# Batch 0's copies, batch 1's scalings and accumulators, and one more filler product in a fused retention and swish kernel

## The chip, the cores and the metric

The kernel runs on one core of a Trainium2 chip. The metric is the device time of one execution in microseconds (us), the median of several runs. Before the change it is 296.62 us over 3 runs (296.17 to 297.3).

Engine names: PE is the matrix engine (PEld its weight loads), DVE, ACT and POOL the vector, scalar and GpSimd engines, SP the engine that issues most DMA. PE writes to PSUM, which has eight banks here divided by tag: three `mm`, two `O`, two `sc`, one `st`.

## The reference

Retention over 8 batches, 8 heads, 576 positions and head size 64, and then a feed-forward with a swish of learned slope:

```
scores = (q @ k^T) / sqrt(64)
gamma[h] = 1 - 2**(-5 - h)
D[h, i, j] = gamma[h]**(i - j) if i >= j else 0
attn = (scores * D) @ v                    # [8, 8, 576, 64]
x = attn.transpose(0, 2, 1, 3).reshape(4608, 512)
h = x @ w_in                               # [4608, 2048]
g = h / (1 + exp(-beta * h))               # beta: one value for each of 2048 columns
out = g @ w_out                            # [4608, 512], float32
```

## The kernel before

**What is computed how.** The decay is split: q is multiplied by gamma**i / 8 (`gq`), v by gamma**-j (`gv`, `gvh`). Positions are taken in chunks of 64. Within a pair of chunks the scores are products of q and k, masked to the causal triangle on DVE (the tiles `R`), then multiplied with v. What lies before a chunk comes in through a state, the running sum of products of k and v (`st` in PSUM, `sbd`, `sbq` and `end` in SBUF). Products of the state with q ("cross" products) are added in the same PSUM tile `O`. The copy of `O` into `xT` is the input of the feed-forward, transposed as PE wants it.

**Blocks.** Each batch gives a block of 512 rows; the last 64 positions of all batches make a ninth block. For each block come `up` (16 groups `fo` of 4 products, then a Silu with slope beta on ACT into `gT`) and `down` (4 row groups `ms` of 16 products, then a copy to `ot` and a store). The Silu of beta * h is beta times too large, so `w_out` is multiplied by 1 / beta (`rbeta_sb`) when it is cast to bfloat16. Before that `betas_safe` (L251) adds 1e-12 to each beta whose square is under 1e-24, in three tiny operations; `tiny` shares its tile with `rbeta_sb`.

**Batch 0** has functions of its own (`pre_q`, `t_q`, `pre_s`, `s_T`, `s_sc`, `s_st`, `s_keep`, `s_O`, `s_cross`, `s_x`), called in the order written out near the end. DVE scales q; PE transposes it; POOL copies or scales k and v, four loads of each; PE transposes k and makes the scores; DVE masks them (L402, eight in all). `s_keep(a, n, ...)` copies a state from PSUM into `sbds[n]` for the head half a, two casts a call, and `s_x(a, hh, e)` copies `O` to `xT` on engine e. Products of the identity with itself (`keep_warm`, L241) and of zeros (`warm_up`) are fillers whose results nobody reads.

**Batch 1** has functions that begin with `o_` and works in two spans of 256 positions, each with heads in two halves a = 0, 1. `o_pre(s, j, a)` makes kn (j = 0) or vn (j = 1), `o_T` transposes kn in PSUM and copies it to kT, `o_sc` makes scores and masks, `o_st(c)` a state's products, `o_keep(c, st)` adds it to the sum before it (L624) and casts that for PE (L629), `o_out` makes the outputs and copies them to xT. Later batches use functions that begin with `d_`, and POOL scales their q.

**Order.** Each engine takes its instructions strictly in the order in which the program emits them. From block 0's feed-forward on, that order is made by `merged`: `fill` is the list of feed-forward steps, and each stream holds (place in `fill`, step) pairs that are put in between. `d0` is the place of block 0's first `down`, `u1` that of block 1's first `up`. There `first_ups` makes two groups with two accumulators in `mm`, and `up(1, 2, ...)` follows with a third. The streams place `pre_q(1, n)`, `t_q(1, u)` and `o_pre` at d0 + 7 to d0 + 12.8, `first_span` at d0 + 14 and `first_out` at d0 + 15.9. `cast_w_in` and `cast_w_out` cast the weights as they land; `rest` holds batch 0's last cross products and copies.

The functions that the change touches, with the line numbers of the profile:

Of the kernel before, what the change touches and what calls it, by code (L numbers as in the profile page):

```python
# [11 lines left out]
F32 = mybir.dt.float32  # L12
BF16 = mybir.dt.bfloat16
ACT = mybir.ActivationFunctionType
ALU = mybir.AluOpType
# [4 lines left out]
def kernel(  # L20
# [10 lines left out]
    nc = tc.nc  # L31
# [4 lines left out]
    P = 128  # L36
# [92 lines left out]

    warm = consts.tile([P, 256], F32, name="warm")  # L130
    first = consts.tile([P, 256], F32, name="first")
    nc.vector.memset(warm[:], 0.0)

    pos = consts.tile([P, 3, CB + 1], F32, name="pos")
    for j, (step, mul) in enumerate(((1, CB), (P, 1))):
# [96 lines left out]
    for g in range(2, NP):  # L232
        load_w_in(g)

    def warm_up(n, cols=256, tag="mm"):
        ph = psum.tile([P, MB], F32, name="ph", tag=tag, bufs=3 if tag == "mm" else 1)
        for _ in range(n):
            src = warm[:].unsqueeze(1).to_broadcast([P, 2, 256]) if cols > 256 else warm[:, :cols]
            nc.tensor.matmul(ph[:, :cols], warm[:, :P], src, start=True, stop=True,
                             skip_group_check=True)  # L240

    def keep_warm(tag="mm"):
# [8 lines left out]

    def betas_safe():

        nc.gpsimd.tensor_tensor(tiny[:], beta_sb[:], beta_sb[:], ALU.mult)
        nc.gpsimd.tensor_scalar(tiny[:], tiny[:], 1e-24, 1e-12, ALU.is_lt, ALU.mult)
        nc.gpsimd.tensor_tensor(beta_sb[:], beta_sb[:], tiny[:], ALU.add)

# [18 lines left out]
    def pre_q(b, n):  # L278

        if n == 0:  # L280
            batch[b] = dict(qs=sb.tile([P, CB, H, D], BF16, name="qs", tag="qs", bufs=2),
                            qT=sb.tile([P, CB, HP, P], BF16, name="qT", tag="qT", bufs=2))
        if b < 2:
            hs, cs = slice(n // 2 * HP, (n // 2 + 1) * HP), slice(n % 2 * 2, n % 2 * 2 + 2)
            for to, hs in [(hs, hs)] if n < 2 or b < QB else turned[1:]:
                nc.vector.tensor_tensor(batch[b]["qs"][:, cs, to], q_tiles[b][:, hs, cs].rearrange("p h i d -> p i h d"),
                                        gq[:, cs, hs].unsqueeze(3).to_broadcast([P, 2, len(range(H)[hs]), D]), ALU.mult)
        else:
            if n % 2:
                return  # L290
            cs = slice(n, n + 2)
            for to, hs in turned:
                nc.gpsimd.tensor_tensor(batch[b]["qs"][:, cs, to], q_tiles[b][:, hs, cs].rearrange("p h i d -> p i h d"),  # L293
                                        gq[:, cs, hs].unsqueeze(3).to_broadcast([P, 2, len(range(H)[hs]), D]), ALU.mult)
# [265 lines left out]
        return lambda: cross(1), evict  # L560


    def o_pre(s, j, a, e=None):

        w, S, e = slice(a * HP, (a + 1) * HP), span_of(1, s), e or nc.gpsimd
        src = span_tiles[1, s, j].rearrange("p h i d -> p i h d")
        if j:
            e.tensor_tensor(S["vn"][:, :, w], src[:, :, w],
                            gvh[:, 2 * s:2 * s + 2, w].unsqueeze(3).to_broadcast([P, 2, HP, D]), ALU.mult)
            return  # L570
        for to, hs in turned[1:] if a else turned[:1]:
            e.tensor_copy(S["kn"][:, :, to], src[:, :, hs])  # L572

    def o_T(s, tags, es):

        S, ts = spans[1, s], []
        for a in range(2):
            if a < len(tags):
                T = psum.tile([P, 2 // len(tags), 2, 2, P], BF16, name="T", tag=tags[a], bufs=3 if tags[a] == "mm" else 2)
            t = T[:, a if len(tags) == 1 else 0]  # L580
            for i in range(2):
                for pl in range(2):
                    nc.tensor.transpose(t[:, i, pl, :], heads(S["kn"][:, i], 2 * a + pl), ident[:])
            ts.append(t)
        for a in range(2):
            es[a](S["kT"][:, :, 2 * a:2 * a + 2], ts[a])
# [19 lines left out]
                    nc.vector.tensor_tensor(S["R"][a][:, j], sc[a][j][:], causal_span[:].unsqueeze(2).to_broadcast([P, 2, 2, P]), ALU.mult)  # L606
        return masks

    def o_st(c):

        S, hh = spans[1, c // 2], c % 2
        st = psum.tile([P, HP, D], F32, name="st", tag="st", bufs=1)
        for i in range(2):
            for p in range(HP):
                for j in range(2):
                    nc.tensor.matmul(st[half(j), p, :], S["kn"][half(hh), i, 2 * p + j, :], S["vn"][half(hh), i, head_of(1, p, j), :],
                                     start=i == 0 and p == 0, stop=True, skip_group_check=True)
        return st
# [12 lines left out]
    def o_out(s):  # L631

        S, seen = spans[1, s], set()
        O = {(hh, y): psum.tile([P, 2, P], F32, name="O", tag="sc" if y else "O", bufs=2) for y in range(2) for hh in range(2)}

        def to(hh, p, x):
            first, o = (hh, p // 2, x) not in seen, O[hh, p // 2][half(x), p % 2, :]
            seen.add((hh, p // 2, x))
            return o, first

        def own(hj):
            for i in range(2):
                for pp in range(2):
                    for y in range(2):
                        for hh, j in hj:
                            p = pp + 2 * y
                            h = head_of(1, p, j)
                            o, first = to(hh, p, h % 2)
                            m = nc.tensor.matmul(o, S["vn"][half(hh), i, h, :], S["R"][y][half(hh), j, i, pp, :],  # L649
                                                 start=first, stop=True, skip_group_check=True)  # L650
                            held_back.append(m)
            return m

        def cross(cj):
            for pp in range(2):
                for y in range(2):
                    for hh, j in cj:
                        c, p = 2 * s + hh, pp + 2 * y
                        o, first = to(hh, p, j ^ y)
                        m = nc.tensor.matmul(s_view(o), sbq[2 * c - 1][half(j), p, :], o_q(c, half(j), p),  # L660
                                             start=first, stop=True, skip_group_check=True)
                        held_back.append(m)
            return m

        def fence(last):
            f = nc.vector.memset(fenced[:], 0.0)
            after(f, last)
            held_back.clear()
            return f

        held_back = []
        if s == 0:
            f = fence(cross([(1, 0), (1, 1)]))
            st = o_st(1)
            own([(0, 0), (0, 1), (1, 1)])
            held_back.clear()
            own([(1, 0)])
        else:
            f = fence(own([(0, 1), (1, 0)]))
            own([(0, 0), (1, 1)])  # L680
            st = o_st(3)
            cross([(0, 0), (1, 1)])
            held_back.clear()
            cross([(0, 1), (1, 0)])
        for m in held_back[:2 + 2 * s]:
            after(m, f)

        def evict():
            for n, ((hh, y), o) in enumerate(O.items()):
                c = 2 * s + hh  # L690
                (dve, act)[n % 2](xt(1)[:, 2 * y:2 * y + 2, :, c * PC:(c + 1) * PC], o.rearrange("k p (i w) -> k p i w", i=CB))
        return evict, st
# [36 lines left out]
    def down(m, ms, f0, fn=4, n0=0, nn=d_model):  # L729
# [3 lines left out]
            pos_[ms] = psum.tile([P, d_model], F32, name="po", tag="mm" if m or ms < 3 else "st", bufs=3 if m or ms < 3 else 1)  # L733
        po = pos_[ms]
        for fo in range(f0, f0 + fn):
            parts = ((0, nn),) if m > 1 or CB * fo + ms < (56 if m else 50) else ((0, nn // 2), (nn // 2, nn))
            for x, y in parts:
                nc.tensor.matmul(po[:, x:y], gT[:, fo, ms, :], w_out_sb[:, fo, n0 + x:n0 + y],  # L738
                                 start=(fo == 0), stop=(fo == FO - 1), skip_group_check=m < 2)
# [28 lines left out]
    def F(f, *a):  # L768
        return lambda: f(*a)
# [1 line left out]

    whole_span, low, high = slice(0, P), half(0), half(1)

    warm_up(2, MB)
    betas()
    betas_safe()
    pre_q(0, 0)
    pre_q(0, 1)
    t_q(0, 0)
# [36 lines left out]
    s_x(0, 0, act)  # L816
    s_cross(3, 0)
    s_st(1, 1, 0, low)
    s_x(0, 1, act)
    s_keep(1, 0, (dve, dve), 1)  # L820
    s_st(1, 0, 1, low)
    s_keep(1, 2, (dve, dve), 0)
    s_O(0, 1, "sc")
    s_O(1, 1, "sc")
    cast_w_in(0, (0, 1), (1,))
    cast_w_in(1, (0, 1), (1,))
    cast_w_in(0, (2, 3), (3,))
# [63 lines left out]
    def first_out():  # L891
        evict, st = o_out(0)
        evict()
        o_T(1, ("mm",), (act, dve))
        o_keep(1, st)

    def second_span():
        masks = o_sc(1)
# [9 lines left out]
    def triangles():  # L908
        for t, pattern in zip(tri, ([[1, CB], [CB, TL // CB]], [[1, TL]])):
            nc.gpsimd.memset(t[:], 1.0)  # L910
            for x in range(2):
# [11 lines left out]
                (d0 + 13.6, F(x_k, XB, 0)),  # L923
                (base[2] - 4.5, F(release, 4)), (base[2] + 10, F(release, 4))],
               [(d0 + 7, F(pre_q, 1, n)) for n in range(4)] + [(d0 + 12.5, F(pre_q, XB, n)) for n in range(4)] + [(d0 + 11.6, F(t_q, 1, 0)), (d0 + 11.6, F(t_q, 1, 1))],
               [(d0 + 8, F(o_pre, 0, 0, 0)), (d0 + 8, F(o_pre, 0, 0, 1)), (d0 + 9, F(o_pre, 0, 1, 0)),
                (d0 + 12.7, F(o_T, 0, ("O", "sc"), (dve, act))), (d0 + 12.8, F(o_pre, 0, 1, 1, nc.vector)),
                (d0 + 14, first_span), (d0 + 15.9, first_out)],
               [(d0 + 10, F(o_pre, 1, 0, 0)), (d0 + 10, F(o_pre, 1, 0, 1)), (d0 + 12, F(o_pre, 1, 1, 0)), (d0 + 12, F(o_pre, 1, 1, 1)),
# [89 lines left out]
```

## Time and profile before

| | |
|---|---|
| median of 3 runs | 296.62 us (296.17 to 297.3) |
| the profiled execution | 296.88 us |
| its span, first to last instruction | 295.1 us |
| PE busy in it | 289.5 us, 3404 products |
| DVE, ACT, POOL busy | 103.1, 145.7, 110.0 us |
| DMA | 53.99 MB, 183 GB/s in the mean |

How to read what follows. The profile is a page of one execution, with views that can be asked for. A line of a timeline is: start and length in us, engine, line of the kernel, operation, tile written<-tiles read, shapes, how many were merged (x8), and in brackets the idle time of the engine before it and what ended that. In the chain of waits, followed back from the last instruction, a line is start, length, and what the time went to. In the list of waits: who waited, for whom, us in total, times, longest. Ends of PE's instructions are modelled, so lines of one engine can overlap by some tenths.

### The profile page before, as it was taken

Reading aid. Unit: us, or ns where it says so; the run is one execution under the profiler, and the core shown is the slowest. Engines: PE = TensorE matmul, PEld = TensorE weight load, DVE = VectorE, ACT = ScalarE, POOL = GpSimd, SP = SyncE. Lnnn points to the kernel's source line nnn. Section 1 sums busy time; section 2 is a strip of 40 time slices with the busy share of each in tenths; the row PEclk is TensorE's granted clock in tenths of the full one; section 3 lists DMA queues with packets and bytes.
Section 4 is the critical chain, followed back from the end, with each engine's and each line's share of the span. In section 5 each row is a group of like instructions: output and inputs, shape, how many; then the busy total and the mean of one; then the engine's idle time right before and its main releaser. Section 6 shows DMA issues by size and latency. Waiting matters only on the chain.

```text
span 295.1 us, 7955 instructions
## 1 busy us (share of the span) xinstructions
PE 289.5 (98%) x3404; PEld 150.0 (51%) x3404; DVE 103.1 (35%) x219; ACT 145.7 (49%) x260; POOL 110.0 (37%) x218
## 2 busy tenths in 40 slices
PE   7999999999999999999999999999999999999995
PEld 3654467875544454455445544554554544444443
DVE  5765566505630651055204520354053500110012
ACT  5566537892377334743473348434770167007600
POOL 5956037945904614271229405764323000000000
PEclk9999999999999999999999999999999999999999
DMA  7999999999999799939999939999997110131011
GB/s 224 305 368 384 378 301 276 213 180 235 198 216 259 188 162 244 252 59 160 211 252 215 187 105 266 183 183 199 210 165 143 73 38 0 36 71 38 0 71 71
DMA packets 119938, 53.99 MB, mean 183 GB/s; under 512 B 93648, under 2 KB 112352, under 8 KB 119904
## 3 DMA queue, kind: packets, MB, share of 16 engines
q1 hardware_dynamic: 119872, 53.49, 81.0%
q8 instruction: 26, 0.43, 0.6%
q14 instruction: 8, 0.07, 0.1%
q10 hardware_dynamic: 32, 0.01, 0.0%
HBM read 36.71 MB, written 9.44 MB: 156 GB/s over the span
## 4 chain that ended last, share of the span: by engine, by line
PE 95%; ACT 1%; DMA 1%; DVE 0%; issue 0%; DVEq 0%
PE po L738 43%; PE ph L703 38%; PE ph L718 4%; PE O L531 2%; PE sc L485 1%; PE O L544 1%; PE st L503 1%; DMA qn<-in_q_dram 1%; PE T L346 1%; ACT sbd L453 1%; PE ph L244 1%; PE sc L399 0%; PE sc L600 0%; PE T L379 0%; ACT xT L425 0%; PE O L649 0%
## 5 line engine op out<-in xcount | busy, mean ns | idle before, releaser
L738 PE MATMUL po<-w_out_sb,gT 128*128 128x512 bf16 (+3 forms) x614 | 128.7, 366 | 0.0
L705 ACT ACTIVATE gT<-ph,beta_sb 128x512 bf16<-128x512 f32 (+1 forms) x143 | 91.1, 645 | 49.2 <-PE ph L703 48.8
L703 PE MATMUL ph<-xT,w_in_sb 128*128 128x512 bf16 (+1 forms) x572 | 113.7, 359 | 0.5 <-ACT gT L872 0.5
L738 PEld LDWEIGHTS <-gT 128*128 128x128 bf16 x614 | 58.0, 98 | 62.8
L703 PEld LDWEIGHTS <-w_in_sb 128*128 128x128 bf16 x572 | 55.5, 98 | 56.1 <-issue 0.8
L745 DVE COPY ot<-po 128x512 f32<-128x512 f32 (+2 forms) x33 | 22.2, 672 | 72.8 <-PE po L738 72.8
L293 POOL TENSOR_TENSOR qs<-qn,gq 128x256 bf16<-128x256 f32 (+1 forms) x36 | 26.3, 757 | 34.2 <-DMA qn<-in_q_dram 33.8
L492 DVE TENSOR_TENSOR R<-sc,tri 128x512 bf16<-128x512 f32 x28 | 17.4, 683 | 60.0 <-PE sc L485 60.0
L322 POOL CAST kn<-kvn 128x128 bf16<-128x128 f32 (+1 forms) x72 | 20.9, 328 | 34.2 <-DMA kvn<-in_k_dram 34.1
L300 POOL TENSOR_TENSOR vn<-kvn,gv 128x512 bf16<-128x512 f32 x24 | 25.0, 1041 | 7.7 <-DMA kvn<-in_v_dram 7.5
L559 ACT CAST xT<-O 128x512 bf16<-128x512 f32 x14 | 7.5, 588 | 32.2 <-PE O L544 32.2
L514 ACT CAST sbd<-warm 128x256 bf16<-128x256 f32 x18 | 7.3, 405 | 25.5 <-DVE warm L511 20.7
L718 PE MATMUL ph<-xT,w_in_sb 128*128 128x512 bf16 x56 | 12.9, 379 | 0.1
L511 DVE TENSOR_TENSOR first<-st,warm 128x256 f32<-128x256 f32 x24 | 10.2, 425 | 2.5
L511 DVE TENSOR_TENSOR warm<-st,first 128x256 f32<-128x256 f32 x18 | 7.6, 422 | 9.6 <-PE st L503 8.4
L559 DVE CAST xT<-O 128x512 bf16<-128x512 f32 x14 | 9.0, 686 | 5.1 <-PE O L544 5.1
L721 ACT ACTIVATE gT<-ph,beta_sb 128x512 bf16<-128x512 f32 x14 | 8.6, 686 | 4.2 <-PE ph L718 4.2
L310 POOL TENSOR_TENSOR kn<-tln,gq 128x128 bf16<-128x128 f32 (+1 forms) x12 | 5.6, 470 | 11.8 <-DMA tln<-in_q_dram 7.0
L210 POOL CAST w_in_sb<-wt 128x256 bf16<-128x256 f32 (+1 forms) x15 | 7.9, 540 | 5.0 <-DMA wt<-in_moe_w_in_dram 4.9
L718 PEld LDWEIGHTS <-w_in_sb 128*128 128x128 bf16 x56 | 5.3, 97 | 6.4 <-issue 0.5
L514 ACT CAST sbd<-first 128x256 bf16<-128x256 f32 x18 | 7.3, 405 | 2.3 <-DVE first L511 0.3
L572 POOL CAST kn<-kvn 128x256 bf16<-128x256 f32 (+1 forms) x6 | 2.9, 516 | 13.3 <-DMA kvn<-in_k_dram 13.3
(117 smaller groups left out, 176.6 us busy)
## 6 DMA issues: line engine op xcount, KB each, us to landing
qn<-in_q_dram SPq DMA_DIRECT2D x16, 512.0 KB, 5.9
kvn<-in_k_dram SPq DMA_DIRECT2D x32, 256.0 KB, 5.9
kvn<-in_v_dram SPq DMA_DIRECT2D x32, 256.0 KB, 5.5
out_dram<-ot SPq DMA_DIRECT2D x31, 256.0 KB, 3.6
wt<-in_moe_w_out_dram SPq DMA_DIRECT2D x8, 512.0 KB, 8.8
wt<-in_moe_w_in_dram SPq DMA_DIRECT2D x5, 512.0 KB, 10.2
wt<-in_moe_w_in_dram SPq DMA_DIRECT2D x6, 256.0 KB, 5.7
tln<-in_q_dram SPq DMA_DIRECT2D x8, 128.0 KB, 3.6
```

The lines of the kernel that those rows point to most:

```text
L293: nc.gpsimd.tensor_tensor(batch[b]["qs"][:, cs, to], q_tiles[b][:, hs, cs].rearrange("p h i d -> p i h d"), gq[:, cs, hs].unsqueeze(3).to_ ...
L300: nc.gpsimd.tensor_tensor(live[i]["vn"], kv_tiles.pop(i)[:, 1], gains(gv, c), ALU.mult)
L322: nc.gpsimd.tensor_copy(kn[:, c % 2, to], t[:, 0, hs])
L492: nc.vector.tensor_tensor(R[x][:, j].rearrange("k c p q -> k (c p) q"), sc[x, j].rearrange("k c p q -> k (c p) q"), mask, ALU.mult)
L511: nc.vector.tensor_tensor(new[:], add, sums[(c - 1) % 2][:], ALU.add)
L514: nc.scalar.copy((sbq[c] if c < NC - 1 else ends[u])[:], new[:])
L559: (nc.scalar.copy if n % 2 else nc.vector.tensor_copy)(x, o)
L703: nc.tensor.matmul(ph, w_in_sb[:, ko, fo * P:(fo + 1) * P], xts[m][:, ko, :, w], start=(ko == 0), stop=(ko == KO - 1))
L705: nc.scalar.activation(gts[m][:, fo, :, w], ph, ACT.Silu, scale=beta_sb[:, fo:fo + 1])
L718: nc.tensor.matmul(phs[f][:], w_in_sb[:, ko, f * P:(f + 1) * P], xts[m][:, ko], start=(ko == 0), stop=(ko == KO - 1))
L738: nc.tensor.matmul(po[:, x:y], gT[:, fo, ms, :], w_out_sb[:, fo, n0 + x:n0 + y], start=(fo == 0), stop=(fo == FO - 1), skip_group_check=m < 2)
L745: (nc.scalar.copy if m == 0 else nc.vector.tensor_copy)(ot, po[:, :nn])
```

## The change

- The warm-up operand is cleared and read in its first 128 columns alone, repeated four times; the product has the same size.
- Behind the transpose of beta stands one more `keep_warm`, where `betas_safe` was called. `betas_safe` goes from POOL to DVE, and to a later place, behind batch 0's last `s_O`.
- In batch 0 `s_x(0, 1)` goes from ACT to DVE, and `s_keep(1, 2)` from DVE to ACT.
- In batch 1 the last quarter of q's scaling (`pre_q(1, 3)`, two operations) goes from DVE to POOL. Of `o_pre(0, 1, 1)`, which DVE did whole, POOL does two of the four heads and DVE the others.
- `o_T` of the second span writes to the bank `st` instead of an `mm` bank, and `o_st(1)` to an `mm` bank instead of `st`. In `first_out`, `o_keep(1, st)` now comes ahead of that `o_T`.
- In block 1's `down`, the products of group fo = 14 for ms = 0 and 1 are no longer split into two of 256 columns.

```diff
@@ -129 +129 @@
-    nc.vector.memset(warm[:], 0.0)
+    nc.vector.memset(warm[:, :P], 0.0)
@@ -232 +232 @@
-    def warm_up(n, cols=256, tag="mm"):
-        ph = psum.tile([P, MB], F32, name="ph", tag=tag, bufs=3 if tag == "mm" else 1)
+    def warm_up(n):
+        ph = psum.tile([P, CB, P], F32, name="ph", tag="mm", bufs=3)
         for _ in range(n):
-            src = warm[:].unsqueeze(1).to_broadcast([P, 2, 256]) if cols > 256 else warm[:, :cols]
-            nc.tensor.matmul(ph[:, :cols], warm[:, :P], src, start=True, stop=True,
+            nc.tensor.matmul(ph[:], warm[:, :P], warm[:, :P].unsqueeze(1).to_broadcast([P, CB, P]), start=True, stop=True,
                              skip_group_check=True)
@@ -251 +250 @@
     def betas_safe():
-        nc.gpsimd.tensor_tensor(tiny[:], beta_sb[:], beta_sb[:], ALU.mult)
-        nc.gpsimd.tensor_scalar(tiny[:], tiny[:], 1e-24, 1e-12, ALU.is_lt, ALU.mult)
-        nc.gpsimd.tensor_tensor(beta_sb[:], beta_sb[:], tiny[:], ALU.add)
+        nc.vector.tensor_tensor(tiny[:], beta_sb[:], beta_sb[:], ALU.mult)
+        nc.vector.tensor_scalar(tiny[:], tiny[:], 1e-24, 1e-12, ALU.is_lt, ALU.mult)
+        nc.vector.tensor_tensor(beta_sb[:], beta_sb[:], tiny[:], ALU.add)
@@ -283 +282 @@
-                nc.vector.tensor_tensor(batch[b]["qs"][:, cs, to], q_tiles[b][:, hs, cs].rearrange("p h i d -> p i h d"),
+                e = nc.gpsimd if b and n == 3 else nc.vector
+                e.tensor_tensor(batch[b]["qs"][:, cs, to], q_tiles[b][:, hs, cs].rearrange("p h i d -> p i h d"),
@@ -560 +560 @@
-    def o_pre(s, j, a, e=None):
-        w, S, e = slice(a * HP, (a + 1) * HP), span_of(1, s), e or nc.gpsimd
+    def o_pre(s, j, a, e=nc.gpsimd):
+        S, w = span_of(1, s), slice(a * HP + (2 if e is nc.vector else 0), (a + 1) * HP - (2 if e is not nc.vector and s == 0 and a else 0))
@@ -576 +576 @@
-                T = psum.tile([P, 2 // len(tags), 2, 2, P], BF16, name="T", tag=tags[a], bufs=3 if tags[a] == "mm" else 2)
+                T = psum.tile([P, 2 // len(tags), 2, 2, P], BF16, name="T", tag=tags[a], bufs=1 if tags[a] == "st" else 2)
@@ -606 +606 @@
-    def o_st(c):
+    def o_st(c, tag="st"):
-        st = psum.tile([P, HP, D], F32, name="st", tag="st", bufs=1)
+        st = psum.tile([P, HP, D], F32, name="st", tag=tag, bufs=3 if tag == "mm" else 1)
@@ -671 +671 @@
-            st = o_st(1)
+            st = o_st(1, "mm")
@@ -733 +733 @@
-            parts = ((0, nn),) if m > 1 or CB * fo + ms < (56 if m else 50) else ((0, nn // 2), (nn // 2, nn))
+            parts = ((0, nn),) if m > 1 or CB * fo + ms < (58 if m else 50) else ((0, nn // 2), (nn // 2, nn))
@@ -771 +771 @@
-    warm_up(2, MB)
+    warm_up(2)
     betas()
-    betas_safe()
+    keep_warm()
@@ -816 +816 @@
-    s_x(0, 1, act)
+    s_x(0, 1, dve)
     s_keep(1, 0, (dve, dve), 1)
     s_st(1, 0, 1, low)
-    s_keep(1, 2, (dve, dve), 0)
+    s_keep(1, 2, (act, act), 0)
     s_O(0, 1, "sc")
     s_O(1, 1, "sc")
+    betas_safe()
@@ -891 +892 @@
         evict()
-        o_T(1, ("mm",), (act, dve))
         o_keep(1, st)
+        o_T(1, ("st",), (act, dve))
@@ -923 +924 @@
-               [(d0 + 8, F(o_pre, 0, 0, 0)), (d0 + 8, F(o_pre, 0, 0, 1)), (d0 + 9, F(o_pre, 0, 1, 0)),
+               [(d0 + 8, F(o_pre, 0, 0, 0)), (d0 + 8, F(o_pre, 0, 0, 1)), (d0 + 9, F(o_pre, 0, 1, 0)), (d0 + 9, F(o_pre, 0, 1, 1)),
                 (d0 + 12.7, F(o_T, 0, ("O", "sc"), (dve, act))), (d0 + 12.8, F(o_pre, 0, 1, 1, nc.vector)),
```

More of the change, by code (lines that the diff above doesn't have):

```diff
@@ L568, in o_pre @@
             e.tensor_tensor(S["vn"][:, :, w], src[:, :, w],
-                            gvh[:, 2 * s:2 * s + 2, w].unsqueeze(3).to_broadcast([P, 2, HP, D]), ALU.mult)
+                            gvh[:, 2 * s:2 * s + 2, w].unsqueeze(3).to_broadcast([P, 2, w.stop - w.start, D]), ALU.mult)
             return
         for to, hs in turned[1:] if a else turned[:1]:
-            e.tensor_copy(S["kn"][:, :, to], src[:, :, hs])
+            nc.gpsimd.tensor_copy(S["kn"][:, :, to], src[:, :, hs])
     def o_T(s, tags, es):
```

## The prediction

> **What bounds the kernel now.** I read the page from the top, then the chain of waits, then the list of who waited for whom on PE, and last the timelines of the two stretches that the change touches.
>
> ```profile
> span 295.1 us, 7955 instructions
> ...
> PE 289.5 (98%) x3404; PEld 150.0 (51%) x3404; DVE 103.1 (35%) x219; ACT 145.7 (49%) x260; POOL 110.0 (37%) x218
> ...
> PEclk9999999999999999999999999999999999999999
> ```
>
> PE is busy for 289.5 of 295.1 us. The other engines are half idle, so what counts is only where PE stands still or works slowly.
>
> ```profile
> PE ph L239 <- DVE warm L132: 1.2, 1, 1.2
> PE ph L703 <- ACT gT L872: 0.5, 1, 0.5
> PE T L346 <- DVE qs L286: 0.4, 1, 0.4
> PE sc L399 <- ACT kT L384: 0.2, 1, 0.2
> ```
>
> These four waits, 2.3 us, are all that the trace puts down to PE. The second (0.5) lies in the middle of the kernel, the others in the first 12 us.
>
> ```profile
> 8.73 0.43 PE T L379 x4
> 9.15 0.85 PE ph L244 x2
> ...
> 10.56 0.34 PE T L379 x4
> ...
> 12.66 0.34 PE st L444 x4
> ...
> 15.24 1.08 ACT xT L425 x2
> ...
> 16.37 1.02 PE ph L718 x4
> ...
> 18.60 1.02 PE ph L718 x4
> ...
> 31.32 10.36 PE po L738 x48
> ...
> 41.69 0.89 PE T L346 x16
> ```
>
> The chain says three things. From 16.37 on PE sets the end, but for the wait on L872. Between 12.66 and 16.37 it runs through ACT instead: state copies, then two copies into xT, which the first product of the feed-forward (L718) needs. And PE is slow at first: a filler product of 128x512 takes 0.43 (two in 0.85 at 9.15), while 48 products of that size at 31.32 take 10.36, or 0.216 each. The page's clock row shows 9 throughout, but by these durations the array runs at half rate until about 10.4. The last 3 us of the span hold the final eviction and store, which the change leaves alone.
>
> **The start, part by part.**
>
> ```profile
> 4.90 2.74 DVE L286 TENSOR_TENSOR qs<-qn,gq 128x512 bf16<-128x512 f32 x4 [1.07 <-DMA qn<-in_q_dram]
> ...
> 5.65 1.21 PE L346 MATMUL T<-ident,qs 128*128 128x128 bf16 x8 [0.40 <-DVE qs L286]
> ...
> 10.68 5.03 DVE L402 TENSOR_TENSOR R<-sc,causal 128x512 bf16<-128x512 f32 x8 [0.79 <-PE sc L399]
> ...
> 15.62 1.20 DVE L453 CAST sbd<-st 64x128 bf16<-64x128 f32 x4
> ...
> 17.76 0.69 DVE L425 CAST xT<-O 128x512 bf16<-128x512 f32 x1 [0.94 <-PE O L421]
> ...
> 18.57 0.25 DVE L835 RECIPROCAL rbeta_sb<-beta_sb 128x16 f32<-128x16 f32 x1
> ...
> 5.61 0.66 POOL L254 TENSOR_TENSOR rbeta_sb<-beta_sb 128x16 f32<-128x16 f32 x1 [1.77 <-ACT beta_sb L250]
> 6.35 0.82 POOL L255 TENSOR_SCALAR rbeta_sb<-rbeta_sb 128x16 f32<-128x16 f32 x1
> 7.26 0.46 POOL L256 TENSOR_TENSOR beta_sb<-beta_sb,rbeta_sb 128x16 f32<-128x16 f32 x1
> 7.67 1.17 POOL L370 CAST kn<-kvn 128x512 bf16<-128x512 f32 x2
> 9.10 2.04 POOL L372 TENSOR_TENSOR kn<-kvn,gvh 128x512 bf16<-128x512 f32 x2 [0.27 <-DMA kvn<-in_k_dram]
> ```
>
> The halved memset starts the warm-up at most 0.27 earlier (its own row lasts that long), at least 0. Either way nothing is gained directly, because PE waits for qs at 5.65 anyhow.
>
> Taking the guard of beta off POOL frees it from 5.61 to 7.72. But what follows hangs on loads: at 9.10 POOL idles for 0.27 until the next piece of k lands, and PE reaches the first transposes of kn at 8.73, after the copy that ends at 7.67 + 0.6 = 8.27. So POOL's gain is 0; without that cover it would be the 0.1 between 8.27 and an earlier load. On DVE the three tiny operations cost 0.25 each by the reciprocal of the same shape, 0.75 together. The lower bound is 0.2, the upper bound POOL's own rows, 1.94.
>
> The copy x(0,1) moves from ACT to DVE. ACT had 15.24 + 1.08 = 16.32. DVE has its eight masks until 15.71, then this copy (0.69, the row at 17.76), so 16.33 or so after the overlap of neighbouring starts: no change for L718 at 16.37. What does change is who sets it. ACT's part now ends at about 15.8, and the eight masks on DVE become the chain: they begin at 10.68 and run without a break worth naming. The two casts of s_keep(1,2) in exchange take 0.55 on ACT after 15.8, and PE asks for them only in the last cross products of half 1, which end before 17.76. Behind the copy on DVE stand two casts (0.6, until 16.9) and the guard (until 17.7). The next copy x(1,1) cannot start before 17.76, when PE's cross products release it, so 0.1 is left and the cost is 0.
>
> The filler behind the transpose of beta costs 0.43 in a gap of 0.40. The first four transposes that follow finish (four take 0.43 at 8.73) before the second qs (each takes 2.74 / 4 = 0.69), so nothing is pushed on. Its value is indirect. The array goes from half to full rate at about 10.4, that is 4.75 us after the gap at 5.65, PE's only idle stretch since 1.25. If unbroken work is what brings full rate, closing the gap moves it to about 1.25 + 4.75 = 6.0. If something else does, it stays. The bounds are therefore 0 and what full rate is worth from 6.0 on. The last four transposes of qs wait for DVE until 4.90 + 2.74 = 7.64, so the gain starts there: they and the filler behind them take 0.34 + 0.22 in place of twice 0.43, then the transposes of kn 0.34 for 0.43 and two fillers 0.43 for 0.85, less what kn's end at 8.27 holds back. Copies of kT and half of the scores lie between; I make it 0.7 at the first mask, and as much at L718, since ACT's part has the room. I take the 0.7, because only the rate differs between the 128x512 rows and all work since 5.65 was unbroken.
>
> [...]
>
> **The middle.**
>
> ```profile
> 48.84 1.03 PE L869 MATMUL ph<-xT,w_in_sb 128*128 128x256 bf16 x8
> 50.33 0.60 PE L703 MATMUL ph<-xT,w_in_sb 128*128 128x256 bf16 x4 [0.45 <-ACT gT L872]
> ...
> 48.27 0.76 DVE L691 CAST xT<-O 128x256 bf16<-128x256 f32 x2 [0.45 <-PE O L649]
> ...
> 49.59 0.42 DVE L586 COPY kT<-T 128x512 bf16<-128x512 bf16 x1 [0.56 <-ACT kT L586]
> 49.93 0.42 DVE L624 TENSOR_TENSOR first<-st,warm 128x256 f32<-128x256 f32 x1
> 50.38 0.29 DVE L629 CAST sbd<-first 128x256 bf16<-128x256 f32 x1
> ```
>
> After the eight products of first_ups PE needs a third mm bank for up(1,2). The transposes of o_T(1) hold one, the two accumulators of first_ups the others, so PE stands 0.45 until ACT's first L872 frees one. In the changed program o_T(1) writes to st, and up(1,2) takes the bank in which o_st(1) was. By the built order it waits for DVE's L624, now ahead of the copy of kT: 48.27 + 0.76 + 0.42 = 49.45, before PE gets there at about 49.88. So the 0.45 goes. The new wait has 0.4 of margin; behind it on DVE stand L629 and then kT, which ends at 49.45 + 0.29 + 0.42 = 50.16. The second half of the scores needs kT after four products (half of the 1.03 for eight) and the first half of the scores, past 49.88 + 0.51 = 50.39. Bounds: 0.45 at best, nothing if the next wait takes its place.
>
> ```profile
> 40.09 1.43 DVE L286 TENSOR_TENSOR qs<-qn,gq 128x256 bf16<-128x256 f32 x4 [0.23 <-DMA qn<-in_q_dram]
> ...
> 41.09 1.58 POOL L572 CAST kn<-kvn 128x512 bf16<-128x512 f32 x3 [12.18 <-DMA kvn<-in_k_dram]
> ...
> 44.77 0.61 POOL L572 CAST kn<-kvn 128x512 bf16<-128x512 f32 x1 [0.93 <-DMA kvn<-in_k_dram]
> 45.60 0.74 POOL L572 CAST kn<-kvn 128x256 bf16<-128x256 f32 x2 [0.23 <-DMA kvn<-in_k_dram]
> ...
> 50.52 3.34 POOL L293 TENSOR_TENSOR qs<-qn,gq 128x256 bf16<-128x256 f32 x5 [0.53 <-DMA qn<-in_q_dram]
> ...
> 43.29 0.61 PE L583 MATMUL T<-ident,kn 128*128 128x128 bf16 x8
> ...
> 45.17 0.42 PE L616 MATMUL st<-vn,kn 64*64 64x64 bf16 x16
> ```
>
> Half of the scaling of q goes to POOL: two operations of 128x256, 3.34 / 5 = 0.67 each. The second half of q lands at about 40.05, so POOL would end at 41.4. But it then runs beside DVE's two. The three casts of kn at 41.09, which overlapped DVE's scaling for 0.43, took 1.58, against 0.61 + 0.74 = 1.35 for the same three later: 0.23 lost in 0.43 of overlap. For 0.7 of overlap I add 0.4, so 41.8. PE's last four of the sixteen transposes (from 41.52, 0.056 each) need it at about 42.15. DVE had it ready at 41.52; so the slack falls from 0.6 to 0.35, and costs 0 as long as PE comes no more than 0.35 earlier. Behind it POOL's three casts end at 41.8 + 1.35 = 43.15 (PE's second half at 43.5), vn at 44.2 (1.02 each for the two at 9.10), and the new half of o_pre(0,1,1), at half of that, at 44.7 (PE's products of its heads at 45.2; DVE's half ends sooner than before). Without the slowing POOL is done by 41.4 and PE may come 0.7 earlier.
>
> [...]
>
> Two products of 128x512 in place of four of 128x256 near the end of block 1's second projection change PE's time by nothing: the pairs are the same columns.
>
> **Sum.** The middle gives 0.45. The start gives 0.7, of which the scaling on POOL lets 0.35 through, since the load that gates it does not move with PE. Together 0.8. The profiled execution took 296.88 (its span and 1.78 around it), so it would take 296.1. It lies 0.26 above the median of 296.62; from that the forecast is 295.8.
>
> **Rivals.** *A, full rate comes when it came.* For it: the gap is only 0.40, and nothing here shows that it matters. Against it: no other idle stretch before 10.4. Then only the middle counts: 296.2.
>
> *B, the same as the forecast, and POOL is not slowed.* For it: POOL's second operation hardly overlaps DVE. Then 0.45 + 0.7: 295.45. An early full rate in most executions, where the shown ones vary (296.17 to 297.3), could add some tenths.
>
> *C, the bank wait only moves.* If L624 came after 49.88, by 0.4 or more than the rows make it, up(1,2) would stand as long as before. With A's start: 296.6.
>
> *D, slower.* The guard on DVE costs what it cost POOL, 1.94 rather than 0.75. It stands ahead of the copy x(1,1), on which the second half of the first products (PE at 18.60, 0.15 after that copy) waits. DVE would be free at 16.9 + 1.94 = 18.84 and not 17.76, and PE would stand 0.9. It decides from a guard of about 1.0. For it: three dependent operations; against it: the reciprocal's 0.25. With A: 296.62 - 0.45 + 0.9 = 297.1.
>
> **Chances.** Forecast 0.45, A 0.25, B 0.15, C 0.08, D 0.07. A measurement of this kernel tells about 0.5% from no change, which is 1.5 us: faster means below 295.1, slower above 298.1. The forecast, A and C lie inside; the lower half of B and the lower edge of the forecast reach below, 0.17 in all. D lies inside too; above 298.1 only one twice as dear would come, 0.03. The range of 295.0 to 296.7 takes in the forecast, A, C and most of B, and leaves out D.
>
> **What would show it.** The filler products behind the transposes of qs at 0.22 rather than 0.43, and the first mask on DVE near 10.0 rather than 10.68, if full rate came early; L718 near 15.7. Its first product released by DVE xT and no longer by ACT. No wait of L703 on L872 near 50, and no other there. PE's last transposes of qs near 42 released by POOL, which shows the cap at work. Wrong would be a wait on x(1,1) near 18.6 (D), a wait of L703 on L624 (C), or a guard of beta above 1 us on DVE.

## The result, and the profile after

| | before | after |
|---|---|---|
| median | 296.69 us (296.17 to 297.3, 12 runs) | 295.94 us (295.5 to 296.55, 12 runs) |
| profiled execution | 296.88 | 296.13 |
| its span | 295.1 | 294.4 |

The ratio is 0.9976, 95% interval 0.9966 to 0.9986, or 0.7 us (0.4 to 1.0). The forecast was 295.8, with 296.1 for the profiled execution. So the sum held; the traces and experiments show that two of its terms were not what I took them for, and that they met at the forecast in part by luck.

The page of after, its head and PE's share:

```profile
span 294.4 us, 7957 instructions
PE 288.5 (98%) x3403; PEld 149.2 (51%) x3403; DVE 104.6 (36%) x219; ACT 145.6 (49%) x261; POOL 110.3 (37%) x218
```

The list of who waited for whom on PE, after:

```profile
PE ph L238 <- DVE warm L132: 1.1, 1, 1.1
PE T L346 <- DVE qs L286: 0.9, 4, 0.2
PE st L444 <- POOL vn L372: 0.2, 1, 0.2
PE sc L600 <- DVE kT L586: 0.2, 1, 0.2
PE T L379 <- POOL kn L372: 0.2, 1, 0.2
```

The wait of L703 on L872 is gone, and a new one stands beside its place: L600 on the copy of kT. At the start PE now waits in more places than before, for q, k and v: it is fast enough there to run up against what it is fed. The wait for vn (L444) is the one that counts, as the chain below shows.

PE's and then DVE's timeline of after, at the start:

```profile
5.05 0.39 PE L243 MATMUL ph<-ident 128*128 128x512 bf16 x1
...
6.48 0.38 PE L243 MATMUL ph<-ident 128*128 128x512 bf16 x1
7.10 0.40 PE L346 MATMUL T<-ident,qs 128*128 128x128 bf16 x4 [0.24 <-DVE qs L286]
...
15.84 0.82 PE L718 MATMUL ph<-xT,w_in_sb 128*128 128x512 bf16 x3
```

```profile
9.77 5.11 DVE L402 TENSOR_TENSOR R<-sc,causal 128x512 bf16<-128x512 f32 x8 [0.47 <-PE sc L399]
14.80 0.68 DVE L425 CAST xT<-O 128x512 bf16<-128x512 f32 x1
...
16.01 0.24 DVE L253 TENSOR_TENSOR rbeta_sb<-beta_sb 128x16 f32<-128x16 f32 x1
16.29 0.32 DVE L254 TENSOR_SCALAR rbeta_sb<-rbeta_sb 128x16 f32<-128x16 f32 x1
16.64 0.17 DVE L255 TENSOR_TENSOR beta_sb<-beta_sb,rbeta_sb 128x16 f32<-128x16 f32 x1
17.25 0.69 DVE L425 CAST xT<-O 128x512 bf16<-128x512 f32 x1 [0.44 <-PE O L421]
```

Full rate is there at 5.05 (before: 10.41, where the trace records the change of the granted clock; after: 5.04). The masks begin at 9.77 and not 10.68, L718 at 15.84 and not 16.37: 0.53 earlier. The guard of beta is done at 16.8, ahead of its next copy.

The masks came 0.91 earlier and L718 only 0.53. The chain that ended last, after, says why:

```profile
3.22 5.82 DMA kvn<-in_k_dram
9.18 2.04 POOL kn L372 x2
11.22 1.01 POOL vn L372
12.27 0.71 PE st L444 x8
...
15.91 0.97 PE ph L718 x4
```

It no longer runs through the masks or a copy into xT: the masks end at 14.88, DVE's copy at 15.48, and PE comes to L718 at 15.84 without a wait. It runs through a load of k, POOL's scaling of kn and vn, which cannot begin before that load lands (9.18; before: 9.10), and PE's own work from L444 on. So the load of k now sets the start. (An earlier load was not tried.)

Batch 1's q after the change, from PE's, DVE's and POOL's timelines:

```profile
41.01 1.20 PE L346 MATMUL T<-ident,qs 128*128 128x128 bf16 x16
```

```profile
40.11 1.18 DVE L286 TENSOR_TENSOR qs<-qn,gq 128x256 bf16<-128x256 f32 x2 [0.22 <-DMA qn<-in_q_dram]
```

```profile
40.22 1.54 POOL L286 TENSOR_TENSOR qs<-qn,gq 128x256 bf16<-128x256 f32 x2 [11.32 <-DMA qn<-in_q_dram]
```

PE comes 0.51 earlier and has to wait inside these transposes (1.20 in place of 1.06). What follows is 0.36 earlier: first_ups start at 48.48 (before: 48.84).

The middle after the change, PE's, DVE's and POOL's timelines:

```profile
48.48 1.03 PE L870 MATMUL ph<-xT,w_in_sb 128*128 128x256 bf16 x8
49.35 0.60 PE L703 MATMUL ph<-xT,w_in_sb 128*128 128x256 bf16 x4
49.88 0.42 PE L600 MATMUL sc<-qT,kT 64*64 64x128 bf16 x16
50.50 0.42 PE L600 MATMUL sc<-qT,kT 64*64 64x128 bf16 x16 [0.20 <-DVE kT L586]
...
55.13 0.64 PE L649 MATMUL O<-R,vn 64*64 64x128 bf16 x32
```

```profile
48.57 0.41 DVE L624 TENSOR_TENSOR first<-st,warm 128x256 f32<-128x256 f32 x1
49.02 1.08 DVE L629 CAST sbd<-first 128x256 bf16<-128x256 f32 x1
50.03 0.41 DVE L586 COPY kT<-T 128x512 bf16<-128x512 bf16 x1
```

```profile
48.92 1.04 POOL L293 TENSOR_TENSOR qs<-qn,gq 128x512 bf16<-128x512 f32 x1 [0.37 <-DMA qn<-in_q_dram]
```

Now L703 starts 0.87 after first_ups; before it was 1.49 (48.84 to 50.33). So the wait removed had cost 0.62, not the 0.45 in its bracket: the bracket counts from the modelled end of a product, which lies some 0.17 behind the point at which the next could have started. The new wait has the same trait. Its bracket says 0.20, but the halves of L600 start 0.62 apart, and 32 of them without a wait take 0.47 from start to start (before: 50.86 to 51.33), a half 0.23. It costs 0.39. Cause of the new wait: the cast L629 took 1.08 where it took 0.29 before, and kT stands behind it. Net, from first_ups to the first L649 of the second span: 6.87 before (48.84 to 55.71), 6.65 after.

Start 0.36, middle 0.22 make 0.58 of the 0.75 us between the two profiled executions. Of the other 0.17, 0.15 lies at one spot: the 64 products of block 2's first projection take 14.13 before (from 82.52) and 13.98 after, because the fifth of them starts 0.36 behind the fourth and not 0.22. The same step of 0.35 or 0.36 stands in the traces of `before` + filler and of the second execution with both waits taken away (below), and not in that of `before` + banks, so it varies between executions and is not shown to be a gain of the change.

### The profile page after: what moved, and what is told of

Its sections match the earlier page's. It is cut to its first block, busy times and chain, and to the rows that moved or that the text cites. A ratio compares the mean times of both kernels' runs of the same rounds, so it can differ in the third digit from the quotient of the medians.

```text
span 294.4 us, 7957 instructions
## 1 busy us (share of the span) xinstructions
PE 288.5 (98%) x3403; PEld 149.2 (51%) x3403; DVE 104.6 (36%) x219; ACT 145.6 (49%) x261; POOL 110.3 (37%) x218
## 4 chain that ended last, share of the span: by engine, by line
PE 94%; DMA 2%; POOL 1%; DVE 1%; SPq 1%; issue 0%; POOLq 0%
PE po L738 43%; PE ph L703 38%; PE ph L718 4%; DMA kvn<-in_k_dram 2%; PE O L531 2%; PE sc L485 1%; PE O L544 1%; PE st L503 1%; POOL kn L372 1%; PE st L444 1%; SPq L102 0%; PE O L413 0%; DVE sbd L629 0%; PE T L346 0%; POOL vn L372 0%; PE sc L600 0%
## 5 line engine op out<-in xcount | busy, mean ns | idle before, releaser
L703 PE MATMUL ph<-xT,w_in_sb 128*128 128x512 bf16 (+1 forms) x572 | 113.5, 358 | 0.0
L703 PEld LDWEIGHTS <-w_in_sb 128*128 128x128 bf16 x572 | 55.7, 98 | 55.1 <-DVE first L511 0.3
L293 POOL TENSOR_TENSOR qs<-qn,gq 128x256 bf16<-128x256 f32 (+1 forms) x36 | 26.3, 758 | 33.8 <-DMA qn<-in_q_dram 33.8
L718 PE MATMUL ph<-xT,w_in_sb 128*128 128x512 bf16 x56 | 12.9, 379 | 0.0
L718 PEld LDWEIGHTS <-w_in_sb 128*128 128x128 bf16 x56 | 5.2, 98 | 6.3 <-issue 0.5
L227 DVE TENSOR_SCALAR w_out_sb<-wt,rbeta_sb 128x512 bf16<-128x512 f32 x13 | 5.9, 484 | 5.1 <-DMA wt<-in_moe_w_out_dram 5.1
```

What stands on the lines that cost most here:

```text
L703: nc.tensor.matmul(ph, w_in_sb[:, ko, fo * P:(fo + 1) * P], xts[m][:, ko, :, w], start=(ko == 0), stop=(ko == KO - 1))
L718: nc.tensor.matmul(phs[f][:], w_in_sb[:, ko, f * P:(f + 1) * P], xts[m][:, ko], start=(ko == 0), stop=(ko == KO - 1))
```

## The experiments

All ratios are to runs of `before` that were measured together with the kernel, with 95% intervals. "Full rate" is the time in the trace at which the granted clock last rises in the start (for the kernel with q on DVE, by the length of its fillers); "L372" is the start of POOL's scaling of kn; "L718" and "middle" (first_ups to L649, as above) are read from PE's timeline of the profiled execution.

| kernel | ratio | full rate | L372 | L718 | middle |
|---|---|---|---|---|---|
| before | 1 | 10.41 | 9.10 | 16.37 | 6.87 |
| after | 0.9976 [0.9966, 0.9986] | 5.04 | 9.18 | 15.84 | 6.65 |
| after, again | 0.9976 [0.9967, 0.9986] | 5.52 | 9.36 | 16.02 | 6.26 |
| before + filler | 0.9996 [0.9985, 1.0008] | 4.44 | 9.36 | 16.23 | 6.87 |
| before + banks | 0.9985 [0.9973, 0.9996] | 10.89 | 9.11 | 16.59 | 6.26 |
| before + copies | 0.9993 [0.9980, 1.0006] | 10.11 | 9.21 | 16.28 | 6.87 |
| before + filler, banks, copies | 0.9972 [0.9961, 0.9982] | 4.42 | 8.87 | 15.54 | 6.46 |
| after, no filler | 0.9979 [0.9968, 0.9990] | 10.62 | 9.48 | 16.43 | 6.25 |
| the same, once more | (one run) | 4.41, lost at 7.82, back at 11.23 | 9.49 | 16.97 | 6.25 |
| after, cast late | 0.9980 [0.9968, 0.9992] | 5.59 | 9.13 | 15.79 | 6.25 |
| after, q on DVE | 0.9971 [0.9957, 0.9984] | about 6.8 | 9.83 | 16.50 | 6.26 |
| after, both | 0.9961 [0.9947, 0.9975] | 10.16 | 9.53 | 16.57 | 6.26 |
| after, both, again | 0.9969 [0.9956, 0.9982] | 6.13 | 9.11 | 15.77 | 6.26 |
| after, both, two more fillers | 0.9964 [0.9950, 0.9978] | 4.34 | 9.05 | 15.72 | 6.26 |

The middle is 6.26 with the new banks, unless the new wait stands in it, and 6.87 without. L718 follows L372: in all seven executions with the copies moved and full rate by 7 it starts 6.66 or 6.67 behind it. In each of these PE waits 0.25 at L444 for POOL's vn and then runs 3.57 to L718 without a wait. So there L718, from 15.54 to 16.50, moves with the landing of k and not with the moment of full rate. Where the copies are moved and full rate came later or was lost, the distance is 6.95 to 7.48, and DVE's copy into xT ends just ahead of L718. With the filler and without the copies it is 6.87, in `before` 7.27.

In the group that gave 0.9971 and 0.9961, 12 of the 25 runs of `before` have a mean granted clock of 0.992 to 0.994, about what one stretch of 3.41 us at half rate leaves (0.993 in the execution of "after, no filler" that lost it from 7.82 to 11.23). Without such runs on either side these two ratios would be 0.9974 and 0.9970.

**The filler alone.**

```diff
     betas()
+    keep_warm()
     betas_safe()
```

> The kernel before with the one filler product behind the transpose of beta and nothing else. Theory 1 (the forecast's: unbroken work brings full rate): products of 128x512 run at 0.22 us from about 5 to 6 us in every execution, the first mask on DVE starts near 9.8 to 10.0 instead of 10.68, and the time falls by about 0.5 us, because batch 1's transposes of q still wait for DVE's scaling at 41.52. Theory 2 (full rate comes at the edge of a window that runs free of the kernel's start, if the window was filled with work): full rate somewhere between 4.6 and 8.0, the median falls by 0.3 to 0.5. Theory 3 (the filler does nothing for the rate): full rate as before at 9 to 12.5 in most executions, and the time within 0.1 of before. The wait of L703 on L872 near 50 stays in all of them.

0.9996: nothing that can be measured. In the trace full rate came at 4.44, before the filler began (4.89), and the masks at 9.79, yet L718 moved by 0.14 only. Two things held it. POOL's L372 began 0.26 later than before, at 9.36. And behind it the chain still runs through ACT, whose two copies into xT end at 16.18. With the copies moved and the same start of L372 (9.36, after again) L718 is at 16.02, so ACT's copies cost 0.21 here, from one execution each.

**The copies alone.**

```diff
-    s_x(0, 1, act)
+    s_x(0, 1, dve)
...
-    s_keep(1, 2, (dve, dve), 0)
+    s_keep(1, 2, (act, act), 0)
```

> The kernel before with the swap of batch 0's copies alone: x(0,1) on DVE, the two casts of s_keep(1,2) on ACT. Forecast's step: no gain where full rate comes late (L718 near 16.4), and where it comes early L718 comes with the masks, near 15.8 instead of the 16.2 of e1, a gain of about 0.4. So the median falls by 0.1 to 0.3. Rival: the copies on DVE delay x(1,1) and the second half of the first products, and the time does not move.

0.9993, with full rate late: nothing that can be measured either. Whether the edits need each other the medians do not show: filler, copies and banks alone multiply to 0.9974, and the three together measured 0.9972 (below).

**The banks alone**: in `before`, `o_st(1)` takes an mm bank, `o_T(1)` the bank st, and `o_keep` comes ahead of it.

```diff
-            st = o_st(1)
+            st = o_st(1, "mm")
...
-        o_T(1, ("mm",), (act, dve))
         o_keep(1, st)
+        o_T(1, ("st",), (act, dve))
```

> The kernel before with the swap of the two banks in batch 1 and o_keep ahead of o_T, nothing else. Forecast's theory: the wait of 0.45 on L872 goes and nothing takes its place, the time falls by 0.45. Rival (the trace of the changed kernel): DVE's cast L629 runs beside POOL's scaling and takes about 1.1 instead of 0.29, the copy of kT behind it ends late, PE waits about 0.2 in the second half of the scores, and the time falls by 0.2 to 0.25. For the start: theory 1 says full rate near 10.4 as in the kernel before, since the gap is still there; theory 2 says between 9.1 and 12.5, or before 5.3 when a window happens to lie wholly in the warm-up of 4 us.

0.9985, that is 0.45 us (0.1 to 0.8). PE's timeline of this kernel:

```profile
49.06 1.03 PE L869 MATMUL ph<-xT,w_in_sb 128*128 128x256 bf16 x8
49.94 0.60 PE L703 MATMUL ph<-xT,w_in_sb 128*128 128x256 bf16 x4
50.47 0.64 PE L600 MATMUL sc<-qT,kT 64*64 64x128 bf16 x32
50.94 0.42 PE L616 MATMUL st<-vn,kn 64*64 64x64 bf16 x16
```

No wait in front of L703 and none within L600: the whole 0.6 of the middle is there. The bank wait did not just move.

**After without the filler**, twice; the second is a single execution, for its trace.

```diff
     betas()
-    keep_warm()
     pre_q(0, 0)
```

> The changed kernel without the one filler product behind the transpose of beta. Theory 1: full rate near 10.4 again, L718 near 16.3 instead of 15.8, the time rises by about 0.4 to 0.5. Theory 2: full rate between 9.1 and 12.5, or before 5.3 in about one execution of six; the median rises by about 0.3 to 0.5. Theory 3: no change of the time beyond 0.1.

> The changed kernel without the filler once more, for a second look at when full rate comes. Theory 1 (the gap of 0.4 decides): at 10.4 to 10.9 as in the three executions with the gap. Theory 2 (windows that run free of the kernel's start): anywhere from 9.1 to 12.5, or before 5.3, and not the same twice.

0.9979 against 0.9976 with it: what the filler adds to the median is lost in the intervals. But the two traces of this one kernel show what the rate went with. PE's timeline of the second execution, and busy times over its stretches between the recorded changes of the clock (columns as the view prints them; the first is PE):

```profile
6.79 0.38 PE L243 MATMUL ph<-ident 128*128 128x512 bf16 x1
...
8.42 0.63 PE L243 MATMUL ph<-ident 128*128 128x512 bf16 x1
```

```profile
core 0: us, PE busy (x) PEld busy (x) DVE busy (x) ACT busy (x) POOL busy (x), PEclk, DMA share, GB/s
1.00:4.41 3.41, 3.29 (x4) 1.18 (x4) 1.81 (x14) 2.73 (x5) 2.39 (x13) 1.00 0.64 211
4.41:7.82 3.41, 1.87 (x15) 0.86 (x14) 2.45 (x4) 1.51 (x4) 0.14 (x1) 1.00 1.14 322
7.82:11.23 3.41, 3.21 (x31) 1.93 (x32) 1.33 (x4) 0.55 (x2) 2.97 (x4) 0.50 1.18 291
```

The clock rose at 4.41, fell at 7.82 and rose at 11.23, twice 3.41 us apart. (The PEclk column shows the half rate, 0.50, only behind the first recorded change.) The stretch ahead of each rise was nearly full of PE's work (3.29 and 3.21 of 3.41), the one ahead of the fall 1.87 of 3.41: q's scaling began at 5.20 (4.76 in the other execution) and PE stood for 1.07 before its transposes. So in this execution the clock changed at edges 3.41 us apart, up behind the two nearly full stretches and down behind the other. The edges do not keep their distance from the kernel's start: in the other execution of the same kernel full rate came at 10.62, 0.61 ahead of the edge at 11.23. This fits theory 2 of the expectations; the times that it gave were the author's estimates.

**Both waits taken away.** Three kernels: L629 behind kT ("cast late"); the last quarter of q back on DVE ("q on DVE"); and the two together.

```diff
-    def o_keep(c, st):
+    def o_keep(c, st, cast=True):
...
-        if 0 < c < CB - 1:
+        if 0 < c < CB - 1 and cast:
...
-        o_keep(1, st)
+        o_keep(1, st, False)
         o_T(1, ("st",), (act, dve))
+        nc.vector.tensor_copy(sbq[3][:], sums[1][:])
```

```diff
-                e = nc.gpsimd if b and n == 3 else nc.vector
+                e = nc.vector
```

> The changed kernel with the cast L629 of o_keep(1) moved behind DVE's copy of kT in first_out. If the cast beside POOL's scaling is what takes back half of the middle's gain: kT ends about 49.4, the wait of 0.20 before the second half of the scores near 50.5 goes, and the time falls by 0.2. Rival: the copy of kT itself runs slowed or waits for ACT's half, and the wait stays at 0.1 to 0.2; then the time stays within 0.1. By theory 1 full rate comes at about 5 to 6 as in the changed kernel, by theory 2 anywhere from 4.6 to 8.0.

> The changed kernel with the last quarter of q's scaling for batch 1 back on DVE; POOL keeps its half of the values. If POOL's scaling caps what the early start brings: DVE has it at about 41.5, the sixteen transposes of q near 41 take 1.06 again instead of 1.20, and where full rate came early the time falls by 0.15 to 0.3; where it came late, nothing. Median 0.1 lower. Rival (the load that both wait for is the cap): no change of the median beyond 0.1.

> The changed kernel with the cast L629 behind the copy of kT and the last quarter of q's scaling back on DVE. If both waits are real and independent, 0.2 to 0.4 below the changed kernel, that is a ratio to before of about 0.9965 to 0.997; if the load of q is the cap and the cast alone counts, as e5.

> The same kernel as e6_both (the cast L629 behind kT, and all of batch 1's q on DVE). Theory: both waits cost something in the median, so it stands 0.1 to 0.4 below the changed kernel of this call. Rival: neither can be seen in the median, difference within 0.1.

Cast late, PE's and DVE's timeline:

```profile
50.05 0.64 PE L600 MATMUL sc<-qT,kT 64*64 64x128 bf16 x32
```

```profile
49.39 0.42 DVE L586 COPY kT<-T 128x512 bf16<-128x512 bf16 x1 [0.23 <-ACT kT L586]
49.73 0.28 DVE L897 CAST sbd<-first 128x256 bf16<-128x256 f32 x1
```

The wait is gone and the middle 6.25. Yet the ratio, 0.9980, can't be told from after's. The wait that it removes is not in every execution (next experiment), and in this one batch 1's transposes of q took 1.42 instead of 1.20, so that part of the start's gain went into them. q on DVE, 0.9971, can't be told from after. Both together gave 0.9961 and 0.9969. Measured on one chip, the medians were 295.52 (both, 8 runs) and 295.75 (after, 12 runs): 0.23 in the direction expected, inside the intervals.

Busy times of the first execution of the kernel with both, and of before, over the two stretches of 3.41 us, the step seen above, ahead of their recorded rise:

```profile
3.33:6.75 3.42, 3.08 (x10) 0.78 (x9) 1.83 (x5) 1.85 (x5) 0.46 (x2) 1.00 1.11 353
6.75:10.16 3.41, 3.41 (x20) 1.77 (x18) 2.14 (x4) 1.38 (x2) 2.00 (x3) 1.00 1.17 290
```

```profile
3.58:7.00 3.42, 3.02 (x12) 0.97 (x10) 2.20 (x5) 1.72 (x4) 1.56 (x3) 1.00 1.11 341
7.00:10.41 3.41, 3.41 (x32) 1.89 (x31) 1.62 (x4) 1.28 (x2) 3.06 (x6) 1.00 1.17 291
```

The filler is in the first kernel, and still the scaling of q began late enough (5.25) to leave PE 0.34 idle: 3.08 of 3.42 did not open the clock, nor did 3.02 in before. The second execution of the same kernel:

```profile
2.72:6.13 3.41, 3.41 (x9) 0.96 (x7) 2.39 (x10) 2.23 (x6) 1.00 (x3) 1.00 1.08 354
6.13:9.54 3.41, 2.89 (x38) 1.43 (x38) 2.27 (x4) 1.38 (x2) 1.80 (x3) 1.00 1.17 290
```

Here the window ended at 6.13 and was full, the filler in it. One kernel, and full rate 4 us apart.

**After again.**

> The changed kernel as it is, a second time, so that its trace can be laid beside the first. If the change's gain is one of copies, scalings and banks, and not of when full rate starts, the ratio to before is again 0.9975, within 0.001, wherever its clock record puts full rate. L600 waits for kT again by about 0.2 if L629 and POOL's L293 again overlap; if L629 takes 0.3 here, there is no wait.

PE's, DVE's and POOL's timeline:

```profile
49.46 0.60 PE L703 MATMUL ph<-xT,w_in_sb 128*128 128x256 bf16 x4
49.99 0.65 PE L600 MATMUL sc<-qT,kT 64*64 64x128 bf16 x32
```

```profile
49.13 0.70 DVE L629 CAST sbd<-first 128x256 bf16<-128x256 f32 x1
```

```profile
48.64 1.04 POOL L293 TENSOR_TENSOR qs<-qn,gq 128x512 bf16<-128x512 f32 x1 [0.31 <-DMA qn<-in_q_dram]
```

The same ratio, without the wait of L600. POOL's L293 hangs on a load and came 0.28 earlier here, so the cast was held for less.

**Filler, banks and copies together**, without the change's other edits (the guard of beta, the splits of q and vn, the unsplit products, the halved operand).

> Before with three things of the change alone: the filler, the copies s_x(0, 1) and s_keep(1, 2), and the banks with o_keep ahead of o_T. Theory that these carry it: as the changed kernel, 0.9975, or 0.1 to 0.2 lower since q's scaling stays on DVE. Rival, that the other edits (guard of beta on DVE, the splits of q and vn, whole products) carry part of it: as the banks alone, 0.9985 or higher.

0.9972: these three carry all that can be measured. Of the others only the split of q was taken out alone (q on DVE). Busy times of this kernel ahead of its change of the clock and behind it:

```profile
1.01:4.42 3.41, 3.17 (x4) 1.18 (x4) 1.94 (x14) 2.74 (x5) 2.37 (x13) 1.00 0.67 216
4.42:7.83 3.41, 2.54 (x21) 1.25 (x20) 2.64 (x4) 1.74 (x4) 2.24 (x4) 1.00 1.14 314
```

The warm-up alone filled 3.17 of the first window and opened the clock; the filler began at 4.88. And 2.54 of 3.41 kept it open.

**Two more fillers** behind the transpose of beta, in the kernel with both.

```diff
     keep_warm()
+    keep_warm()
+    keep_warm()
     pre_q(0, 0)
```

> both_again with two more fillers behind the transpose of beta. Theory that full rate follows from windows of 3.41 us full of PE's work: in nearly every execution PE does not idle before qs, so full rate comes by 8.5 at the latest; it saves 0.1 to 0.3 of the median where loads of q land late, and costs at most as much where they do not, so the ratio is within 0.001 of both_again. Rival, that full rate does not follow from PE's idle time: full rate near 10 in the trace, as in e6_both.

0.9964 (5 runs), not to be told from 0.9961 and 0.9969. Full rate came at 4.34, before the fillers (4.78), so this trace does not test them.

## Why the prediction was right, and where it was not

- **The middle.** "So the 0.45 goes" held, and rival C (the wait only moves to L624) fell: L703 waited in none of the kernels with the new banks. Two sizes were off. The wait was worth 0.62, since I took the bracket and not the distance between starts. And kT came at 50.44 instead of 50.16, because I took L629 for 0.29: in the trace of before it ran ahead of POOL's scaling, in the new order it runs into it. The forecast named kT as next in line behind the wait, but gave the row no upper bound. Without the wait the term is 0.61, with it 0.22; 0.45 lies between.
- **The start: two steps failed.** The first: "If unbroken work is what brings full rate, closing the gap moves it to about 1.25 + 4.75 = 6.0." Full rate was early in the profiled execution, as forecast, but the change came at 5.04, before the filler (5.05) had done anything. By the traces it depends on where the edges 3.41 us apart fall (4.41, 7.82 and 11.23 in one execution, 10.62 in another of the same kernel), and how full of work the stretch ahead of each is (3.02 and 3.08 us did not open the clock, 3.17 and more did). The filler's part is smaller: it helps where an edge falls so that it lies in the window, as at 2.72 to 6.13 above. That the filler opened the clock there is inferred: without its 0.5 us that window would be no fuller than those that did not open.
- The second step: "I make it 0.7 at the first mask, and as much at L718, since ACT's part has the room." It was 0.91 at the mask and 0.53 at L718. The prediction had read that POOL hangs on a load of k at 9.10, and put its gain at 0; it did not follow that row on to vn and L444, where it becomes the limit as soon as PE is faster. The sign "first product released by DVE xT" did not come for the same reason.
- Of the profiled executions with the filler, 8 of 9 had full rate by 7; of those without it, 4 of 5 had it after 10 and one lost it again. In the median the filler came to 0.1 us (0.9979 against 0.9976). Whether it is worth more than that, intervals of 0.3 us to each side leave open.
- The runs without a trace say something too, since their mean granted clock is on record. It is 0.992 to 0.994 in 27 of 121 runs without the filler and in 7 of 92 with it, and in the three groups of `before` such runs were 0.40 to 0.46 us longer in the median than the rest. From these figures I estimate that keeping the rate is worth under 0.1 us in the mean. That it is the filler that keeps it is not shown: the kernels differ in more, and in `before` alone the share went from 4 of 35 to 12 of 25.
- **Rival A** (full rate when it came) is not dead but the case in some executions: 10.16 in one of the kernel with both.
- **The copies.** Costed at nothing: no cost shows. That with them the masks become the chain holds only where full rate is late. Where it is early, the load of k sets the end, and the copies are worth 0.21 (16.23 and 16.02, both with L372 at 9.36).
- **POOL's scaling of q.** Forecast to end at 41.8, it ended at 41.76, and let 0.36 through of 0.51, where I had 0.35 of 0.7. Rival B (not slowed, 41.4) fell in this execution. Of the 0.36 that it came later than B's 41.4, the load made 0.17 (start 40.22, not 40.05) and the slowing 0.2, half of what I had added. DVE's two beside it, which I had left as they were, took 1.18 in place of 0.72 (half of 1.43). Both were slowed in the overlap, POOL by 0.2 and DVE, the more, by 0.46.
- **The guard** ended 0.8 after its start (forecast 0.75, D from 1.0 on). D fell: the copy x(1,1) began at 17.25.
- **Transposes and the clock.** The prediction counted the transposes of qs into the unbroken work. The one window that tells bears this out: 6.75 to 10.16 opened the clock with twelve whole transposes in it, which took 1.4 us of its 3.41 in that kernel's timeline. The rest, 2.0, is less than the 3.02 to 3.08 that did not open it elsewhere.

So 0.8 was a sum of a middle that is larger (0.6 less what L629 takes) and a start that is 0.4 in some executions and nothing in others, by when k and q land as much as by the rate. That the two met at the forecast is in part luck. The banks alone measured 0.45 us (0.1 to 0.8); filler and copies alone gave 0.1 and 0.2, neither clear of nothing; and all three together 0.8 (0.5 to 1.2).

## What to carry to other kernels

The cost of a wait is the distance between the starts around it, against the same distance where nothing waits; the bracket leaves out the tail of the product before (0.62 against a bracket of 0.45 here, 0.39 against 0.20). An operation that moves past a wait also moves beside other engines' work: take its duration from a row with that neighbour, or bound it by the neighbour's whole length (L629 took 0.29 ahead of POOL's scaling, 1.08 beside it). Before a gain is put down to a filler, compare two executions of one kernel (full rate at 10.16 and at 6.13 here). And when a chain is shortened, follow the engines that stood just beside it: one that hangs on a load and costs nothing today, as POOL here (its L372 from 9.10), can be the next limit.

## What the runs showed of the hardware

- **A cast on DVE beside POOL ended only after POOL's instruction.** L629 reads and writes SBUF alone. Where POOL's scaling had started before it, the cast behind L624 ended 0.14 to 0.15 us after POOL's instruction in all ten such executions, and took 0.35 to 1.08 us; where it started first or alone it took 0.28 or 0.29 (four executions). In after: POOL until 49.96, the cast until 50.10. L624, with an input from PSUM, kept its 0.41 beside POOL (after again: 48.68, POOL from 48.64). By these times what the overlap cost was the rest of POOL's instruction. What holds the cast is not shown.
- **What opened and closed the clock.** Windows in which PE was busy 3.02 (`before`) and 3.08 us (after, both) of 3.42 did not open it; 3.17 (before + filler, banks, copies), 3.29 (after, no filler, once more) and 3.41 of 3.41 (after) did. Once open it stayed through 2.54 of 3.41 (before + filler, banks, copies) and was lost after 1.87 (after, no filler, once more). What lies between was not measured.
- **Runs of one kernel spread by about 1 us**, with the filler (295.5 to 296.55) and without it (295.48 to 296.63). Full rate moves by 4 us between executions of one kernel, the start of L372 by up to 1.0 between all of them (8.87 to 9.83); how much of the spread each makes was not measured.
